# Chunk 0's queries and keys laid out by pairs of token blocks, in a new order of the pieces

## The chip, the cores and the metric

The kernel runs on one core of a Trainium2 chip. The metric is the device time of one execution in microseconds (us). The engines are TensorE (PE, its weight loads PEld), VectorE (DVE), ScalarE (ACT), GpSimd (POOL) and the DMA queues, which SP, ACT and POOL feed.

## What is computed

The input is one sequence of S = 2048 tokens with D = 640 features. It is normalized once, and two branches read the result: a sliding attention of 32 heads of 20 features, in which a token looks at itself and at 7 earlier tokens, each two positions further back (W = 8, dilation 2), and a feed-forward net of 1536 units with GELU. Both results and x are added.

```python
xn = layernorm(x)                                   # no gain or bias
q, k, v = split(xn @ wqkv)                          # 32 heads of 20
idx = pos[:, None] - 2 * arange(8)[None, :]         # masked where idx < 0
logits = einsum("bhsd,bhswd->bhsw", q, k[idx]) * 20 ** -0.5
attn = softmax(where(idx >= 0, logits, -1e9))
A = einsum("bhsw,bhswd->bhsd", attn, v[idx]) @ wo
B = gelu(xn @ w1 + b1) @ w2 + b2
out = x + A + B
```

## The kernel before

**Tiling.** Tokens are handled in 4 chunks of 512 (n = 0 to 3), each of 4 blocks of 128 (j or bl). Features lie on the 128 partitions in KT = 5 tiles. Everything is bfloat16 except sums in PSUM and the softmax. Queries, keys and values of a chunk are tiles [128, 5, 512], keys and values with 14 leading columns (PAD) more, which hold the last columns of the chunk before (zeros in chunk 0).

**Attention of a chunk.** VectorE multiplies queries with shifted keys: `qk n j h` (L402) handles token block j and four of the eight shifts (half h), writing `half0` or `half1`, 2560 elements per partition. The keys are read through a hand-made access pattern (`window`) that steps back by two columns from shift to shift. TensorE sums the products over the features of each head (`lg n`, L443) into the PSUM tile L, VectorE takes the maximum (`m`) and subtracts it (`mx`), ScalarE takes the exponential (`ex`), VectorE sums, inverts and multiplies (`ss`, `ri`, `at`). DMAs spread the weights over the partitions (`xd n` issued by SP for blocks 0 and 1, `xs n` by ScalarE for blocks 2 and 3). VectorE multiplies them with the values (`av n j h`) and adds up (`ad n`, `ot n`). In chunks 2 and 3 `pa` adds pairs of feature tiles first.

**Feed-forward net and output.** `f1n_t` (L549) is the first layer for unit tile t into a PSUM buffer, `ge n_t` its GELU on ScalarE. `o n bl pc` (L585, L587) is the output of a block: pc 0 to 3 from the net, pc 4 from the attention (`ot` must be done). `oc` copies it out of PSUM, `od` adds it to the output by a POOL DMA. The last block's output is added by VectorE and stored by SP and ACT.

**Chunk 0.** Its projections come in parts. `ga`, `gb`, `gd` make the queries of blocks 0 and 1, copied by `gc`. `hj w p g` makes queries, keys or values (w = 0, 1, 2) of pair p of token blocks (pair 0 is blocks 0 and 1) for feature tiles 0-1, 2-3 or 4 (g = 0, 1, 2), ten matmuls or five; `hc w p g` (L372) copies it out on ScalarE. In the other chunks a projection `pj n w t` is five matmuls of 512 columns, copied by `pc`. `pad n w` copies the leading columns.

**Normalization.** `st` are statistics on VectorE (chunks 0, 1); `su`, `ng`, `sq` do the same on ScalarE (chunks 2, 3). `rs` is the root on ScalarE, `rc` the reciprocal on VectorE, `xn` the normalized block, `tp`/`tc` its transpose (chunk 0 on TensorE; for the others `tc` is a DMA transpose on the SP queue). `ldx`, `ld2`, `ldo` are later loads on SP, `xp` copies x to the output, `xb` adds the bias there.

**Order.** The text `ORDER` lists all pieces in one line of time. Each engine of PE, DVE, ACT and SP executes its own pieces strictly in that order; waits between engines are found from the data, tile by tile and range by range. The pool `psA` has four PSUM buffers for `hj`, `pj`, `f1` (and for part of the last chunk's output): a buffer comes free when ScalarE has copied it out. L has one buffer, and so has each half of the output (`lo`, `hi`). ScalarE loads a function table (L167) whenever the next function is of another kind: root, exponential, GELU.

Of the kernel before, what the change touches and what calls it, by code (L numbers as in the profile page):

```python
# [13 lines left out]
BF16 = mybir.dt.bfloat16  # L14
F32 = mybir.dt.float32

S, D, F, H, W, DIL = 2048, 640, 1536, 32, 8, 2
P = 128
DH = D // H
PAD = (W - 1) * DIL  # L20
KT, FT = D // P, F // P
CH = 512
# [14 lines left out]

ORDER = """
pad01 pad02 st00a st00 sum1 rs00 mean1 neg1 rc00 sq1 xn00a xn00b tp00a wa tp00b wb tc00a rs01 ga tc00b rc01 xn01 gb2
tp01 gb3 tc01a tc01b gb4 gd gc0 ge tb b1 ho hj102 st02a gc1 st03a hc102 gc4 st02 rs02 st03 hj100 rs03 rc02 hc100 rc03  # L40
xn02 xn03 hj101 st12a hc101 st11a st13a hj201 st10a tp02 tc02 tp03 hj200 tc03 st11 hc201 hc200 hj202 hc202 hj012 hj110
hc110 st12 st13 st10 rs1 hc012 qk001 hj010 hc010 hj111 rc1 xn12 qk000 qk011 qk010 xn11 hj011 hc011 tc12 tc11 hj112
hc111 hc112 f10_1 ge0_1 qk020 xn13 tc13 qk030 f10_11 qk031 f10_6 ge0_6 xn10 f10_0 ge0_0 pad11 f10_9 hj211 hc211 ge0_9
f10_2 hj212 qk021 lg0 hc212 ge0_11 tc10 pj103 ge0_2 pc103 mask m0 mx0 ex0 ss0 pj114 pj101 pc101 pj104 pc104 pj111
pj113 pc114 pj112 pj102 pc111 ri0 ldx ld2 su23 pj100 pc113 pj110 at0 su21 pc112 su20 f11_0 pc102 pc100 pc110 qk110
qk101 qk130 f11_7 qk111 qk131 qk120 qk100 f10_4 xd0 su22 ng2 ge1_7 sq20 f11_3 ge1_3 ge1_0 f10_5 sq22 qk121 pj122 ge0_5
sq21 ldo ge0_4 hj210 xp0 xs0 f10_3 ge0_3 pj121 sq23 rs2 rc2 o000 o001 lg1 hc210 av010 av000 m1 xn21 f10_7 tc21 pc122
f11_9 av001 xn22 av030 tc22 mx1 pc121 ge0_7 f10_10 ge0_10 f10_8 pj123 xn20 tc20 ge0_8 xn23 ge1_9 f11_10 f11_5 ge1_5
o002 pj120 av020 av021 ex1 ss1 pc120 xp1 av031 ri1 pj124 pc124 o003 av011 pad21 tc23 pj213 pc213 pc123 pj202 pc202
pj211 pc211 pj214 pc214 at1 pj222 pad12 ge1_10 pc222 pj204 pj224 pc224 xs1 pj200 ad01 ad00 pc200 pj201 su31 ad02 ot0  # L50
xd1 pc201 pj210 pc210 av111 av110 su30 pj223 pc223 av131 av101 f11_4 pc204 pj203 f12_9 su32 pc203 xb1 su33 av130 pj221
pc221 o004 oc00 xb0 od00 pj220 pc220 o020 av121 o021 o022 o023 o024 ng3 sq31 sq30 sq32 oc02 f11_2 av120 av100 sq33 rs3
rc3 xn33 tc33 od02 xn30 o030 o031 o032 o033 ad10 tc30 o034 oc03 pj212 o010 ge1_4 ad11 ad12 o011 o012 o013 o014 xn31
tc31 f11_6 pc212 qk221 xn32 ge1_2 ot1 qk201 qk200 f12_4 ge2_4 qk210 qk211 qk230 qk231 ge1_6 pa210 oc01 qk220 pa211
pa200 pad22 f11_1 ge1_1 f12_11 ge2_11 pa201 tc32 pj314 pc314 pj300 pc300 pj303 pc303 pj301 pc301 ge2_9 pj304 pc304
pj311 pj302 pj313 pc313 pc302 pj312 pc312 f13_8 pj310 f13_10 pad31 pc310 f13_6 xl lg2 ge3_8 m2 mx2 ge3_10 pc311 ge3_6
o130 qk300 ex2 ss2 f13_5 f11_8 ge1_8 od03 f12_7 o131 qk310 ri2 ge2_7 pa300 at2 qk301 f12_1 pj324 qk321 qk331 qk311
ge3_5 f11_11 ge1_11 pa311 ge2_1 f13_11 o132 o133 pc324 f12_0 ge2_0 qk330 pj321 f13_1 xs2 qk320 pa310 f13_7 ge3_1 ge3_7
xp2 pj320 f13_9 ge3_9 o134 oc13 pc321 pc320 ge3_11 pj323 pc323 o110 pa301 o111 o112 lg3 m3 av230 av231 o113 od01 o114
oc11 mx3 pad32 av221 ex3 ss3 xd2 av210 ri3 av201 pj322 pc322 f13_0 at3 f13_3 ge3_3 o100 od11 o101 f12_5 o102 o103 o104  # L60
oc10 f13_2 o120 o121 xs3 ge3_2 av211 o122 av200 av220 ad21 ge2_5 od13 f12_6 ge3_0 o123 o124 xb2 xb3 ad20 f12_3 ad22
ot2 f12_2 oc12 ge2_6 ge2_2 f12_8 ge2_8 ge2_3 od12 f13_4 f12_10 o310 av321 ge3_4 o220 o221 o222 ge2_10 o223 o224 oc22
od10 od22 o330 o311 xd3 o200 o201 av330 o202 o203 av300 o204 oc20 od20 o331 o332 o210 o211 o212 o213 o214 oc21 av310
o312 o230 o231 o232 o233 o234 o313 av311 av331 av320 av301 ad31 ad30 ad32 oc23 ot3 o320 o321 o322 o323 o324 o314 od21
oc32 od23 o300 o301 o302 o303 o304 oc31 od32 o333 o334 od31 oc30 od30 oclo ohi ochi ochd
""".split()


# [1 line left out]
def kernel(  # L70
# [16 lines left out]
    nc = tc.nc  # L87
# [14 lines left out]
    qkvp = ctx.enter_context(tc.tile_pool(name="qkvp", bufs=2))  # L102
    prodp = ctx.enter_context(tc.tile_pool(name="prodp", bufs=1))
    smp = ctx.enter_context(tc.tile_pool(name="smp", bufs=1))
# [33 lines left out]
    for c in range(2):  # L138
        cs = slice(c * F // 2, (c + 1) * F // 2)
# [31 lines left out]
    mask = consts.tile([H, W, MW], BF16, name="mask")  # L171
# [20 lines left out]
    tiles = {}  # L192

    def get(key, make):
        if key not in tiles:
            tiles[key] = make()
        return tiles[key]
# [107 lines left out]
    def qkv_tile(n, which):  # L305
        if which == 0:
            return get(("q", n), lambda: qkvp.tile([P, KT, CH], BF16, tag="qT", name="qT"))
        tag = "kT" if which == 1 else "vT"
        return get((tag, n), lambda: qkvp.tile([P, KT, PAD + CH], BF16, tag=tag, name=tag))

    wqkv_p = [w[:].rearrange("p t (c r) -> p t r c", r=KT) for w in wqkv]

# [13 lines left out]
    def bank(key):  # L326
        return get(("bank", key), lambda: psA.tile([P, BPC, P], F32, tag="acc", name="gps"))
# [20 lines left out]
                q_piece(1, to, ti, ti == 0 and to == 0, ti == KT - 1 and to >= BPC - 1)  # L348

    def do_gc(g):  # L350
        q = qkv_tile(0, 0)
        if g == BPC:
            nc.scalar.copy(q[:, BPC, 0 : 2 * P].rearrange("p (b m) -> p b m", b=2), bank(BPC)[:, 0:2, :])
        else:
            nc.scalar.copy(q[:, 0:BPC, g * P : (g + 1) * P], bank(g)[:])
# [12 lines left out]
                )  # L368

    def do_gq(which, pair, a, b):  # L370
        off = (PAD if which else 0) + pair * 2 * P
        nc.scalar.copy(qkv_tile(0, which)[:, a:b, off : off + 2 * P], tiles["pair", which, pair, a][:, 0 : b - a, :])  # L372

    def do_pc(n, which, to):
        dest = qkv_tile(n, which)
        off = 0 if which == 0 else PAD
        nc.scalar.copy(dest[:, to, off : off + CH], tiles["pps", n, which, to][:])  # L377

    def do_pad(n, which):
        dest = qkv_tile(n, which)  # L380
        if n == 0:
            nc.gpsimd.memset(dest[:, :, 0:PAD], 0.0)
        else:
            nc.scalar.copy(dest[:, :, 0:PAD], qkv_tile(n - 1, which)[:, :, CH : CH + PAD])


    half = [prodp.tile([P, W // 2, KT, CH], BF16, name=f"half{i}") for i in range(2)]

    def window(src, h, cs):

        first = PAD - DIL * (W // 2 * h) + cs.start
        row = src[:, :, first : first + cs.stop - cs.start]
        (part, n_part), (tile_step, n_tile), (_, n_col) = row.ap
        return bass.AP(
            tensor=row.tensor,
            offset=row.offset,
            ap=[[part, n_part], [-DIL, W // 2], [tile_step, n_tile], [1, n_col]],
        )

    def do_qk(n, j, h):  # L400
        cs = slice(j * P, (j + 1) * P)
        nc.vector.tensor_tensor(  # L402
            out=half[h][:, :, :, cs],
            in0=qkv_tile(n, 0)[:, :, cs].unsqueeze(1).to_broadcast([P, W // 2, KT, P]),
            in1=window(qkv_tile(n, 1), h, cs),
            op=ALU.mult,
        )

# [75 lines left out]
            nc.vector.tensor_tensor(out=a[:, 0:k, :], in0=a[:, 0:k, :], in1=a[:, k : 2 * k, :], op=ALU.add)  # L484

    def do_recip(n):
        rs = smp.tile([P, P], F32, tag="rs", name="rs")
        tiles["rs", n] = rs
        nc.vector.reciprocal(rs[:], tiles["ss", n][:, 0, :])

# [133 lines left out]
    def piece(name, fn, *args):  # L624
        assert name not in pieces
        pieces[name] = lambda: fn(*args)

    for name in "tb b1 mean1 ho ldx ld2 ldo xl oclo ohi ochi ochd mask".split():
        piece(name, locals()[f"do_{name}"])
    for u, a, b, eng, own in (("a", 0, 2, "ve", "lo"), ("b", 2, KT, "se", "hi")):  # L630
        piece(f"xn00{u}", do_xn, 0, 0, a, b)
# [24 lines left out]
    for g in (0, 1, BPC):  # L656
        piece(f"gc{g}", do_gc, g)
    for which in range(3):
        for pair in range(0 if which else 1, 2):
            for g, (a, b) in enumerate(COLS):  # L660
                piece(f"hj{which}{pair}{g}", do_gp, which, pair, a, b)
                piece(f"hc{which}{pair}{g}", do_gq, which, pair, a, b)
    for n in range(NCH):
# [18 lines left out]
        for which in (1, 2):  # L682
            piece(f"pad{n}{which}", do_pad, n, which)
# [3 lines left out]
        for h in range(2):  # L687
            for j in range(BPC):
                piece(f"qk{n}{j}{h}", do_qk, n, j, h)
                piece(f"av{n}{j}{h}", do_av, n, j, h)  # L690
            if n in PAIRED:
                for c in range(2):
                    piece(f"pa{n}{h}{c}", do_pa, n, h, c)
        piece(f"lg{n}", do_lg, n)
        for name, fn in (("m", do_max), ("mx", do_sub), ("ex", do_exp), ("ss", do_sum), ("ri", do_recip), ("at", do_attn)):
            piece(f"{name}{n}", fn, n)
# [54 lines left out]
```

## Time and profile before

| quantity | value |
|---|---|
| median of 3 runs | 215.12 us (214.79 to 215.48) |
| the profiled execution | 215.14 us |
| its span, first to last instruction | 212.6 us |
| TensorE busy | 205.3 us (97%) |
| VectorE busy | 174.2 us (82%) |
| ScalarE busy | 126.3 us (59%) |
| mean granted TensorE clock | 0.998 |

The span is counted from the first instruction; some 2.5 us of the profiled execution's time lie outside it. Busy shares are averages over the span. In timeline rows the columns are start, duration, engine, line, operation, tiles, shape, count, and in brackets the idle time ahead with what ended it. Rows of one group overlap a little where an engine starts the next instruction before the last has fully ended, so the step from start to start is shorter than the duration of one.

### The profile page before, as it was taken

Reading aid. Unit: us, or ns where it says so; the run is one execution under the profiler, and the core shown is the slowest. Engines: PE = TensorE matmul, PEld = TensorE weight load, DVE = VectorE, ACT = ScalarE, POOL = GpSimd, SP = SyncE. Lnnn points to the kernel's source line nnn. Section 1 sums busy time; section 2 is a strip of 40 time slices with the busy share of each in tenths; the row PEclk is TensorE's granted clock in tenths of the full one; section 3 lists DMA queues with packets and bytes.
Section 4 is the critical chain, followed back from the end, with each engine's and each line's share of the span. In section 5 each row is a group of like instructions: output and inputs, shape, how many; then the busy total and the mean of one; then the engine's idle time right before and its main releaser. Section 6 shows DMA issues by size and latency. Waiting matters only on the chain.

```text
span 212.6 us, 3291 instructions
## 1 busy us (share of the span) xinstructions
PE 205.3 (97%) x1327; PEld 114.6 (54%) x1349; DVE 174.2 (82%) x162; ACT 126.3 (59%) x241; POOL 19.8 (9%) x37
## 2 busy tenths in 40 slices
PE   8999799999999999999999999999999999999993
PEld 3999355545445555555545544544555555555552
DVE  3498885639889999999999969996999999999001
ACT  5576686989998778678875477435462641111120
POOL 2000000000200200110110000006101101111121
PEclk9999999999999999999999999999999999999999
DMA  6992248977692395024611000396924611122253
GB/s 213 390 396 83 63 63 256 363 165 245 111 173 65 123 174 147 0 34 62 111 19 28 0 0 0 62 274 124 192 44 72 166 21 12 22 31 34 31 62 62
DMA packets 24069, 23.89 MB, mean 112 GB/s; under 512 B 9080, under 2 KB 21880, under 8 KB 24056
## 3 DMA queue, kind: packets, MB, share of 16 engines
q1 hardware_dynamic: 17008, 14.68, 23.5%
q0 software_dynamic: 4144, 4.92, 17.9%
q10 hardware_dynamic: 2904, 4.10, 6.4%
q8 instruction: 10, 0.16, 0.3%
q14 instruction: 3, 0.02, 0.0%
HBM read 10.00 MB, written 7.54 MB: 82 GB/s over the span
## 4 chain that ended last, share of the span: by engine, by line
PE 86%; DVE 8%; ACT 3%; issue 1%; DVEq 0%
PE lo L585 26%; PE pps L318 22%; PE hps L549 19%; DVE half L402 8%; PE hi L587 8%; PE gps L362 4%; PE L L443 3%; PE idle L415 2%; PE gps L331 1%; ACT hT L565 1%; ACT xn L257 1%; PE tp L274 1%; ACT L167 1%; ACT kT L372 0%; ACT kT L377 0%
## 5 line engine op out<-in xcount | busy, mean ns | idle before, releaser
L549 PE MATMUL hps<-xnT,w_sb 128*128 128x512 bf16 x237 | 55.6, 379 | 1.8 <-ACT kT L372 1.4
L402 DVE TENSOR_TENSOR half<-qT,kT 128x2560 bf16<-128x2560 bf16 x32 | 45.8, 1486 | 5.3 <-ACT kT L377 3.6
L585 PE MATMUL lo<-w_sb,hT 128*128 128x512 bf16 x136 | 39.7, 379 | 0.1
L549 PEld LDWEIGHTS <-w_sb 128*128 128x128 bf16 x240 | 23.0, 98 | 28.7 <-issue 2.9
L587 PE MATMUL hi<-w_sb,hT 128*128 128x128 bf16 x144 | 31.5, 219 | 0.5 <-issue 0.2
L592 ACT CAST osb<-lo 128x512 bf16<-128x512 f32 x15 | 8.8, 585 | 39.1 <-issue 19.9
L565 ACT ACTIVATE hT<-hps,b1T 128x512 bf16<-128x512 f32 x36 | 23.9, 684 | 8.9 <-PE hps L549 8.9
L528 DVE TENSOR_TENSOR half<-vT,ax 128x2560 bf16<-128x2560 bf16 x16 | 23.1, 1476 | 1.5 <-PE L L443 1.5
L598 POOL DMA_DIRECT2D out_dram<-osb x15 | 13.0, 864 | 118.6 <-ACT osb L593 106.7
L585 PEld LDWEIGHTS <-hT 128*128 128x128 bf16 x144 | 14.1, 98 | 17.5 <-issue 0.8
L528 DVE TENSOR_TENSOR half<-vT,x_sb 128x2560 bf16<-128x2560 bf16 x16 | 22.6, 1484 | 0.0
L585 PE MATMUL lo<-wo,oT 128*128 128x512 bf16 x76 | 22.4, 379 | 0.0
L537 DVE TENSOR_TENSOR half<-half,half 128x5120 bf16<-128x5120 bf16 x8 | 22.2, 2820 | 0.1
L167 ACT ACT_TABLE_LOAD x14 | 18.0, 1283 | 1.0 <-PEq L735 0.7
L318 PE MATMUL pps<-xnT,wv_sb 128*128 128x512 bf16 x73 | 18.2, 379 | 0.1
L318 PE MATMUL pps<-xnT,wk_sb 128*128 128x512 bf16 x75 | 18.0, 379 | 0.1
L318 PE MATMUL pps<-xnT,wq_sb 128*128 128x512 bf16 x72 | 17.4, 379 | 0.1
L587 PE MATMUL hi<-wo,oT 128*128 128x128 bf16 x80 | 16.9, 219 | 0.2
L587 PEld LDWEIGHTS <-hT 128*128 128x128 bf16 x144 | 14.1, 98 | 1.7
L585 PEld LDWEIGHTS <-oT 128*128 128x128 bf16 x80 | 7.8, 98 | 9.4
L318 PEld LDWEIGHTS <-wq_sb 128*128 128x128 bf16 x75 | 8.7, 118 | 7.6 <-issue 0.4
L318 PEld LDWEIGHTS <-wk_sb 128*128 128x128 bf16 x75 | 8.7, 118 | 7.3
(86 smaller groups left out, 267.0 us busy)
## 6 DMA issues: line engine op xcount, KB each, us to landing
w_sb<-in_B_w_dram SPq DMA_DIRECT2D x4, 960.0 KB, 10.8
out_dram<-osb POOLq DMA_DIRECT2D x15, 160.0 KB, 3.4
out_dram<-b2bc POOLq DMA_DIRECT2D x3, 640.0 KB, 6.8
x_sb<-in_A_x_dram SPq DMA_DIRECT2D x1, 1280.0 KB, 6.0
out_dram<-x_sb ACTq DMA_DIRECT2D x1, 1120.0 KB, 4.9
ax<-attn SPq DMA_DIRECT2D x4, 256.0 KB, 4.0
ax<-attn ACTq DMA_DIRECT2D x4, 256.0 KB, 4.2
x_sb<-attn SPq DMA_DIRECT2D x4, 256.0 KB, 4.7
```

Source lines behind the costliest of these rows:

```text
L167: nc.scalar.activation(warm[:], nc.const_aps.tensor(0.0, [P, 1], F32), func)
L318: nc.tensor.matmul(ps[:], lhsT=wqkv_p[which][:, ti, to, :], rhs=xnT[:, ti, :], start=(ti == 0), stop=(ti == KT - 1),)
L362: nc.tensor.matmul(ps[:, to - a, :], lhsT=wqkv_p[which][:, ti, to, :], rhs=tiles["xnT", 0][:, ti, pair * 2 * P : (pair + 1) * 2 * P], star ...
L402: nc.vector.tensor_tensor(out=half[h][:, :, :, cs], in0=qkv_tile(n, 0)[:, :, cs].unsqueeze(1).to_broadcast([P, W // 2, KT, P]), in1=window ...
L528: nc.vector.tensor_tensor(out=half[h][:, :, :, cs], in0=window(qkv_tile(n, 2), h, cs), in1=ax_view(n)[:, j, ws, :].unsqueeze(2).to_broadca ...
L537: nc.vector.tensor_tensor(out=a, in0=a, in1=b, op=ALU.add)
L549: nc.tensor.matmul(ps[:], lhsT=w1_sb[:, ti, ft * P : (ft + 1) * P], rhs=tiles["xnT", n][:, ti, :], start=(ti == 0), stop=(ti == KT - 1),)
L565: nc.scalar.activation(hT, tiles["hps", n, ft][:], ACT.Gelu_apprx_tanh, bias=b1T[:, ft : ft + 1], scale=1.0)
L585: nc.tensor.matmul(lo[:], lhsT=lhs, rhs=rhs[:, 0:CH], start=first, stop=last)
L587: nc.tensor.matmul(hi[:, 0 : D - CH], lhsT=lhs, rhs=rhs[:, CH:D], start=first, stop=last)
L592: nc.scalar.copy(osb[:, 0:CH], tiles["lo", n, bl][:])
L598: nc.gpsimd.dma_start(rows, tiles["osb", n, bl][:], accum_op=ALU.add)
```

## The change

In chunk 0 the query tile is read as two ranges, one for each pair of token blocks, [128, 5, 256] each. The key tile becomes two ranges of [128, 5, 14 + 256], each with leading columns of its own; those of pair 1 are a copy of the last 14 columns of pair 0, made by the new piece `pk` on ScalarE. `qk` of chunk 0 reads queries and keys from the range of its pair. The tiles of the other chunks are laid out as before. The reciprocal's tile takes the tag, and so the buffer, of the maximum. The order of the pieces is new throughout.

```diff
 ORDER = """
 pad01 pad02 st00a st00 sum1 rs00 mean1 neg1 rc00 sq1 xn00a xn00b tp00a wa tp00b wb tc00a rs01 ga tc00b rc01 xn01 gb2
-tp01 gb3 tc01a tc01b gb4 gd gc0 ge tb b1 ho hj102 st02a gc1 st03a hc102 gc4 st02 rs02 st03 hj100 rs03 rc02 hc100 rc03
-xn02 xn03 hj101 st12a hc101 st11a st13a hj201 st10a tp02 tc02 tp03 hj200 tc03 st11 hc201 hc200 hj202 hc202 hj012 hj110
-hc110 st12 st13 st10 rs1 hc012 qk001 hj010 hc010 hj111 rc1 xn12 qk000 qk011 qk010 xn11 hj011 hc011 tc12 tc11 hj112
-hc111 hc112 f10_1 ge0_1 qk020 xn13 tc13 qk030 f10_11 qk031 f10_6 ge0_6 xn10 f10_0 ge0_0 pad11 f10_9 hj211 hc211 ge0_9
-f10_2 hj212 qk021 lg0 hc212 ge0_11 tc10 pj103 ge0_2 pc103 mask m0 mx0 ex0 ss0 pj114 pj101 pc101 pj104 pc104 pj111
-pj113 pc114 pj112 pj102 pc111 ri0 ldx ld2 su23 pj100 pc113 pj110 at0 su21 pc112 su20 f11_0 pc102 pc100 pc110 qk110
-qk101 qk130 f11_7 qk111 qk131 qk120 qk100 f10_4 xd0 su22 ng2 ge1_7 sq20 f11_3 ge1_3 ge1_0 f10_5 sq22 qk121 pj122 ge0_5
-sq21 ldo ge0_4 hj210 xp0 xs0 f10_3 ge0_3 pj121 sq23 rs2 rc2 o000 o001 lg1 hc210 av010 av000 m1 xn21 f10_7 tc21 pc122
...
+tp01 gb3 tc01a tc01b gb4 gd gc0 ge tb b1 st03a gc1 hj101 hj100 hj202 st02a hc101 st03 rs03 st02 rs02 gc4 hc100 hj201
+ho rc03 hc202 rc02 xn02 xn03 tp02 tc02 tp03 st12a st11a hj200 hj102 st13a st10a tc03 st13 hc201 hc102 hj010 pk st12
+hj012 hc200 hc010 st11 hj011 st10 rs1 hc012 qk001 rc1 qk000 hc011 qk010 qk011 hj112 hc112 xn12 tc12 xn13 tc13 hj110
+hc110 hj111 hc111 qk020 qk021 f10_6 ge0_6 xn11 tc11 f10_0 f10_2 f10_9 f10_1 ge0_0 hj212 ge0_9 f10_11 xn10 tc10 ge0_2
+ldx hj211 qk030 ld2 qk031 lg0 hc212 hc211 pad11 ge0_1 pj100 ge0_11 pc100 mask m0 mx0 ex0 ss0 ri0 pj102 pc102 pj112
+pc112 pj101 pj111 pc101 pj104 at0 pj103 pj114 su20 su21 pc104 pc111 su22 pj110 pc114 pc110 pc103 pj113 pc113 qk130
+qk100 qk111 qk120 qk131 qk101 qk110 qk121 xs0 pj124 pc124 su23 hj210 hc210 pj121 pc121 f11_9 ng2 sq20 pj122 pc122 sq21
+sq23 pj120 pj123 f10_5 ldo o000 pc123 sq22 pc120 rs2 rc2 f10_7 f10_10 lg1 m1 av031 xd0 av001 av011 av000 mx1 ge0_5
+av030 xn23 tc23 ge0_7 f10_4 xn22 tc22 f10_3 ge0_4 ge0_10 ge0_3 xn20 tc20 ge1_9 xn21 f10_8 ge0_8 f11_5 ge1_5 f11_10
+pad21 ge1_10 av010 f11_0 ge1_0 ex1 ss1 av021 ri1 o001 f11_7 o002 tc21 av020 xp1 pj203 pc203 su33 pj211 at1 xp0 xd1
+pj201 pj202 ad00 pc211 pc201 f11_3 ge1_3 pj214 pc214 o003 ge1_7 pad12 pj213 pc213 ad01 ad02 ot0 pj212 pc212 av101
+pj224 pc224 pj222 xs1 pj204 pc204 pc222 pad22 av110 pj220 pj210 av131 pc220 su30 av100 xb0 av111 av121 av120 xb1 pc210
+pj223 av130 su31 su32 ng3 pj200 pc202 sq32 f12_2 o004 oc00 od00 sq33 pj221 pc223 pad31 o020 o021 o022 pc200 pc221 sq30
+o023 o024 oc02 sq31 rs3 rc3 xn31 tc31 f12_11 xn32 ad10 tc32 o030 o031 o032 o033 o034 oc03 f11_6 ad11 ad12 qk211 o010
+o011 o012 o013 o014 f12_4 ge2_11 ot1 qk221 qk231 qk201 qk200 xn33 tc33 xn30 qk220 qk230 qk210 ge2_2 pa201 ge2_4 ge1_6
+f11_11 pa200 f11_2 ge1_2 tc30 pj311 pj302 pc302 pj304 pc311 ge1_11 pa211 pa210 pj310 pj312 pc312 pj323 pc323 pj300
+pc304 pj314 pc314 pj313 pc313 pc310 od03 pj303 f13_0 pj301 pc300 f13_5 xl pc301 pc303 pj321 lg2 m2 pc321 ge3_5 ge3_0
+oc01 od01 f11_4 ge1_4 qk321 mx2 f11_1 qk320 od02 ge1_1 ex2 f11_8 ss2 f13_8 ge1_8 pj324 pj320 o130 ge3_8 f12_1 ri2 at2
+xd2 o131 f12_9 ge2_9 qk310 o132 o133 o134 qk311 ge2_1 qk301 xs2 qk331 pa310 oc13 od13 f13_11 qk300 f13_4 qk330 ge3_4
+ge3_11 o110 o111 o112 o113 pa300 pj322 o114 pa301 pc320 oc11 f12_0 pa311 lg3 m3 mx3 ex3 av231 xp2 ss3 o100 o101 o102
+o103 o104 pc322 pc324 oc10 f12_5 ri3 at3 xd3 f13_6 ge3_6 o120 ge2_5 f13_2 f12_6 ge2_0 f13_10 o121 o122 od10 f13_1 o123
+o124 av220 av201 xb2 xb3 ge3_1 ge3_2 av200 oc12 od12 f13_9 ge3_9 ge3_10 ge2_6 f12_8 ge2_8 xs3 f13_3 ge3_3 av221 av211
+av210 f12_7 ge2_7 av230 f12_10 f12_3 ge2_3 f13_7 ge3_7 o220 o330 ad20 o331 pad32 ad21 ad22 o221 o222 ot2 av331 ge2_10
+o223 o224 oc22 od22 o310 o230 o231 o232 o233 o234 av320 oc23 av330 av300 av301 av311 o311 od11 o200 o201 o202 o203
+o204 av321 oc20 od20 o312 o210 o211 o212 o213 o214 oc21 av310 ad30 od21 ad31 o313 o320 o321 o322 ad32 ot3 o323 o324
+od23 o314 oc32 o300 o301 o302 o303 o304 od32 o332 o333 o334 ohi oc31 od31 oc30 oclo ochi ochd od30
 """.split()
...
@@ -305,8 +305,20 @@
     def qkv_tile(n, which):
         if which == 0:
             return get(("q", n), lambda: qkvp.tile([P, KT, CH], BF16, tag="qT", name="qT"))
-        tag = "kT" if which == 1 else "vT"
-        return get((tag, n), lambda: qkvp.tile([P, KT, PAD + CH], BF16, tag=tag, name=tag))
+        if which == 2:
+            return get(("vT", n), lambda: qkvp.tile([P, KT, PAD + CH], BF16, tag="vT", name="vT"))
+        flat = get(("kT", n), lambda: qkvp.tile([P, 2 * KT * (PAD + 2 * P)], BF16, tag="kT", name="kT"))
+        return flat[:, 0 : KT * (PAD + CH)].rearrange("p (t m) -> p t m", t=KT)
+
+    def pair_of(which, pair):
+
+        if which == 0:
+            return qkv_tile(0, 0)[:].rearrange("p t m -> p (t m)")[:, pair * KT * 2 * P : (pair + 1) * KT * 2 * P].rearrange(
+                "p (t m) -> p t m", t=KT
+            )
+        qkv_tile(0, 1)
+        size = KT * (PAD + 2 * P)
+        return tiles["kT", 0][:, pair * size : (pair + 1) * size].rearrange("p (t m) -> p t m", t=KT)
 
     wqkv_p = [w[:].rearrange("p t (c r) -> p t r c", r=KT) for w in wqkv]
 
@@ -348,7 +360,7 @@
                 q_piece(1, to, ti, ti == 0 and to == 0, ti == KT - 1 and to >= BPC - 1)
 
     def do_gc(g):
-        q = qkv_tile(0, 0)
+        q = pair_of(0, 0)
         if g == BPC:
             nc.scalar.copy(q[:, BPC, 0 : 2 * P].rearrange("p (b m) -> p b m", b=2), bank(BPC)[:, 0:2, :])
         else:
@@ -368,8 +380,13 @@
                 )
 
     def do_gq(which, pair, a, b):
-        off = (PAD if which else 0) + pair * 2 * P
-        nc.scalar.copy(qkv_tile(0, which)[:, a:b, off : off + 2 * P], tiles["pair", which, pair, a][:, 0 : b - a, :])
+        if which == 2:
+            off = PAD + pair * 2 * P
+            dest = qkv_tile(0, which)[:, a:b, off : off + 2 * P]
+        else:
+            off = PAD if which else 0
+            dest = pair_of(which, pair)[:, a:b, off : off + 2 * P]
+        nc.scalar.copy(dest, tiles["pair", which, pair, a][:, 0 : b - a, :])
 
     def do_pc(n, which, to):
         dest = qkv_tile(n, which)
@@ -377,11 +394,16 @@
         nc.scalar.copy(dest[:, to, off : off + CH], tiles["pps", n, which, to][:])
 
     def do_pad(n, which):
-        dest = qkv_tile(n, which)
+        dest = pair_of(1, 0) if (n, which) == (0, 1) else qkv_tile(n, which)
         if n == 0:
             nc.gpsimd.memset(dest[:, :, 0:PAD], 0.0)
+        elif (n, which) == (1, 1):
+            nc.scalar.copy(dest[:, :, 0:PAD], pair_of(1, 1)[:, :, 2 * P :])
         else:
             nc.scalar.copy(dest[:, :, 0:PAD], qkv_tile(n - 1, which)[:, :, CH : CH + PAD])
+
+    def do_pk():
+        nc.scalar.copy(pair_of(1, 1)[:, :, 0:PAD], pair_of(1, 0)[:, :, 2 * P :])
 
 
     half = [prodp.tile([P, W // 2, KT, CH], BF16, name=f"half{i}") for i in range(2)]
@@ -399,10 +421,13 @@
 
     def do_qk(n, j, h):
         cs = slice(j * P, (j + 1) * P)
+        q, k, at = qkv_tile(n, 0), qkv_tile(n, 1), cs
+        if n == 0:
+            q, k, at = pair_of(0, j // 2), pair_of(1, j // 2), slice(j % 2 * P, (j % 2 + 1) * P)
         nc.vector.tensor_tensor(
             out=half[h][:, :, :, cs],
-            in0=qkv_tile(n, 0)[:, :, cs].unsqueeze(1).to_broadcast([P, W // 2, KT, P]),
-            in1=window(qkv_tile(n, 1), h, cs),
+            in0=q[:, :, at].unsqueeze(1).to_broadcast([P, W // 2, KT, P]),
+            in1=window(k, h, at),
             op=ALU.mult,
         )
 
@@ -484,7 +509,7 @@
             nc.vector.tensor_tensor(out=a[:, 0:k, :], in0=a[:, 0:k, :], in1=a[:, k : 2 * k, :], op=ALU.add)
 
     def do_recip(n):
-        rs = smp.tile([P, P], F32, tag="rs", name="rs")
+        rs = smp.tile([P, P], F32, tag="m", name="rs")
         tiles["rs", n] = rs
         nc.vector.reciprocal(rs[:], tiles["ss", n][:, 0, :])
 
@@ -625,7 +650,7 @@
         assert name not in pieces
         pieces[name] = lambda: fn(*args)
 
-    for name in "tb b1 mean1 ho ldx ld2 ldo xl oclo ohi ochi ochd mask".split():
+    for name in "tb b1 mean1 ho ldx ld2 ldo xl oclo ohi ochi ochd mask pk".split():
         piece(name, locals()[f"do_{name}"])
     for u, a, b, eng, own in (("a", 0, 2, "ve", "lo"), ("b", 2, KT, "se", "hi")):
         piece(f"xn00{u}", do_xn, 0, 0, a, b)
```

## Prediction

> **What bounds the kernel now.** I read the page first (busy shares, then the chain that ended last), then TensorE's own waits, then the stretches of five microseconds, and at the one place that stood out the timeline.
>
> ```profile
> span 212.6 us, 3291 instructions
> PE 205.3 (97%) x1327; PEld 114.6 (54%) x1349; DVE 174.2 (82%) x162; ACT 126.3 (59%) x241; POOL 19.8 (9%) x37
> ...
> PE 86%; DVE 8%; ACT 3%; issue 1%; DVEq 0%
> ```
>
> TensorE is busy for 97% of the span and carries 86% of the chain. The change adds and removes no matmul, so only time in which TensorE stands still can be won, and any new standstill is lost in full. TensorE's list of waits names one that matters:
>
> ```profile
> PE hps L549 <- ACT kT L372: 1.4, 1, 1.4
> ```
>
> The stretches put it early; from 35 us to 205 us TensorE is full:
>
> ```profile
> 20.00:25.00 5.00, 3.67 (x23) 2.31 (x23) 4.37 (x4) 2.76 (x5) 0.00 (x0) 1.00 0.29 66
> 25.00:30.00 5.00, 4.74 (x25) 2.55 (x25) 4.67 (x4) 4.97 (x9) 0.00 (x0) 1.00 0.14 34
> ...
> 35.00:40.00 5.00, 5.00 (x25) 2.70 (x23) 3.48 (x5) 4.46 (x8) 0.00 (x0) 1.00 1.06 394
> ```
>
> (Columns: stretch, its length, busy time of PE, PEld, DVE, ACT, POOL, then granted clock.) The timeline of that place shows the cause:
>
> ```profile
> 18.42 1.49 DVE L402 TENSOR_TENSOR half<-qT,kT 128x2560 bf16<-128x2560 bf16 x1 [0.83 <-ACT kT L372]
> 20.11 4.29 DVE L402 TENSOR_TENSOR half<-qT,kT 128x2560 bf16<-128x2560 bf16 x3
> 21.87 0.56 ACT L372 CAST qT<-gps 128x512 bf16<-128x512 f32 x1
> 24.44 0.86 ACT L372 CAST kT<-gps 128x512 bf16<-128x512 f32 x2 [2.01 <-DVE half L402]
> 25.07 3.60 PE L549 MATMUL hps<-xnT,w_sb 128*128 128x512 bf16 x15 [1.35 <-ACT kT L372]
> 25.33 5.70 DVE L402 TENSOR_TENSOR half<-qT,kT 128x2560 bf16<-128x2560 bf16 x4 [0.93 <-ACT kT L372]
> 31.92 2.34 PE L443 MATMUL L<-half,head_of 128*32 128x512 bf16 x40
> ```
>
> The first four products (`qk001` to `qk010`) read keys of pair 0. They end at 24.40, and only then may ScalarE write the keys of pair 1 (`hc111`, `hc112`), which they do not need. The pairs' columns alternate in memory for all five tiles, so the reader's span covers the other pair. While `hc111` waits, ScalarE passes nothing on, the four PSUM buffers fill, and TensorE stops for 1.35 us. Likewise the first product waits 0.83 us, until `hc110` ends at 18.31. The queries show no such link: at 21.87 ScalarE writes queries of pair 1 in the middle of three products. So the keys' layout does the work, and the queries' layout I cost at nothing.
>
> **The wait removed.** On TensorE, from 9.84 to the first matmul of `lg0` at 31.92, 22.08 us pass. Starts lie 0.216 us apart at 512 columns, 0.109 at 256, 0.056 at 128 (five of 512 make the 1.08 us steps of the chain; thirty of 256 take 3.29). Ahead of `lg0` stand 9 pieces hj of ten matmuls (9 x 1.093 = 9.84), 5 of five (2.73), 10 transposes (0.56) and 6 FFN pieces (6 x 1.079 = 6.47): 19.60 us. So 22.08 - 19.60 = 2.48 us are waits. The new order has the same pieces ahead of `lg0`, differently sorted, so it can start at 9.84 + 19.60 + 0.09 (entry, as before) = 29.53, if two others keep up.
>
> VectorE: its statistics end at 17.59 as before. `hc102`, now the last copy that `qk001` needs, ends at about 16.45 (its matmuls end at 15.87), so `qk001` starts at 17.6. With a step of 1.41 us per product and 0.3 for `rc1`, the eighth ends at 29.3, against 31.02; `qk020` wants `hc111`, due at 22.3, at 23.6. ScalarE: copies step by 0.5, `xn` by 0.81, GELUs by 0.58, a table load with its warm-up by 1.40. Its queue then reads `hc112` 19.7, `xn12`, `xn13` 21.3, `hc110`, `hc111` 22.3, table and `ge0_6` 24.3, `xn11`, `ge0_0` 25.7, `ge0_9` 26.4, `xn10`, `ge0_2` 27.8. Each frees a PSUM buffer 0.5 to 1.3 us before TensorE wants it. The transpose `tc10` can be issued at 27.3, its data wanted at 31.8; transposes landed in 2.4 to 4.5 us. So 2.39 us come off.
>
> **Small parts.** `pk`, one copy of 128x70, is added to ScalarE: 0.24 us by the same-sized copy at 30.05. Behind it stand `hc200` and `hc010`, whose buffers are wanted 0.9 us later or more; it is covered, and without that cover costs 0.24. Maximum and reciprocal in one buffer: both are written and read by VectorE alone, and in its queue `mx` precedes `ri` and `at` precedes the next `m`, so nothing waits. Product speed: 1.486 us for 2560 elements before. Rows now lie 270 elements apart instead of 526. The nearest slow row is a subtraction of float32, 1.23 us for 1024 elements, which scaled gives 3.1. The value rows, of the other 526-element tile, also take 1.48, so I keep 1.49. The Trainium skill (VectorE: DVE Perf Modes, "Mode 2×_1P") asks for 16-bit data, step one and 4-byte alignment; rows of 540 bytes and a pair offset of 2700 bytes still satisfy that, so by its rule this term is nought too; did it fail, the sum would go to the last rival below.
>
> A removed TensorE pause might also pay in clock. The granted clock stays 1.00 through the 1.35 us pause, and the next matmuls start 0.216 apart, so I count no such gain.
>
> **Does the rest of the order keep 2.39 us?** I moved all marks by that much and added up queue by queue. `lg1` needs `qk121`. TensorE reaches it at 54.2, VectorE delivers at 54.7: a stall of 0.3, as before (56.47 against 57.15). From the end of `lg1`, VectorE needs 26.9 us to `ot0` (2 x 1.14 for m and mx, 8 x 1.41, 1.38, 0.88, 1.13, three adds of 2.78, 1.41), and TensorE has 27.6 us ahead of `o004`: no stall. `lg2`: halves 120.8, TensorE 121.1. `lg3`: 145.0 against 145.3. `o224`: `ot2` 173.7 against 174.5. `o324`: `ot3` 194.8 against 196.3; TensorE then has 10.7 us left. All are met, by 0.3 to 1.5 us. Thinner places are PSUM buffers behind ScalarE. `pj210` needs `pc204`, now queued behind the two DMA issues of `xs1` (2.02 us before): 0 to 0.6, I take 0.1. `f12_1` needs `ge1_8`, behind `ex2` and two table loads: 0 to 0.7, I take 0.2, as sums meet within that. `f13_7` needs `ge3_3`, behind the issues of `xs3` (2.63 us before): 0 to 1.3, I take 0.3, since issues partly overlap ScalarE's work at 51.67. `pj203` needs transpose `tc21`, due at 64.8 to 66.9, wanted at 66.2: 0 to 0.7, I take none, as the median landing is 2.5. On SP, `ldo` now precedes `xd0` and `xp0` follows the transposes; both are wanted 10 us later than issued. The last store moves with TensorE's end: `od30` is issued 3.3 us ahead of it instead of 2.7, so it cannot be last. Given back: 0.6.
>
> Sum against the profiled execution, 215.14 us (span 212.6 and 2.5 around it; the median of three is 215.12): 215.14 - 2.39 + 0.6 = 213.35, say 213.3. The thin places at their dear ends (0.6 + 0.7 + 1.3 + 0.7 = 3.3 instead of 0.6) would give 216.0, but they do not add up, since a TensorE late at one finds the next buffer free. One or two of them give 214.4. At their cheap ends, with `lg1` unstalled, it is 212.5.
>
> **Rivals.** *Gain eaten*: the later stages take the 2.4 us back in several tie places, 214.5 to 215.7, centre 215.1. For it: six ties within half a microsecond. Against: VectorE idles for 1.64 and 2.13 us ahead of its third and fourth maximum already, and a late TensorE relaxes every tie.
>
> *ScalarE falls behind around `lg1`* (the one that ends slower): `f11_9`, `f10_5`, `f10_7` and `f10_10` hold all four PSUM buffers when `lg1` starts, and `ge0_5`, which frees the first, stands behind four squares, six copies, the root's table and the GELU table. At the steps above ScalarE is through `ge0_4` at 58.9, wanted by `f10_8` at 59.2. At full row durations (copies 0.59, squares 0.83 + 0.20, sums 0.95, GELUs 0.69, xn 0.92, DMA issues 2.63 for 1.25) the same list is 3.65 us longer, TensorE loses 3.3, and the time is 216.6. It decides against the change once ScalarE needs 2.75 us more than my steps. Against it: the steps come from back-to-back runs of the same instructions, and fourteen table loads have a mean of 1.283 us.
>
> The Trainium skill (ScalarE: Activation LUTs, "Rules for kernel authors") speaks against this place: it budgets some 2.7 us for every switch to another table set. With two switches in that list its figure, an estimate here, would add 2.6 us to ScalarE, and the sum would be 215.6 instead of 213.3; I keep the trace's 1.28 and the warm-up behind it.
>
> *The link stays*: if the two key pairs are still held to touch, `hc112` waits for `qk011` (23.7 instead of 19.4), `hc111` ends at 26.9, the products at 32.6, `lg0` starts 3.2 us later than I say, and the time is 216.5. Against it: the pairs now lie in two ranges that do not meet.
>
> *Products slow down*: eight at 3.1 instead of 1.49 make `lg0` 13 us later: 226.
>
> **How the numbers follow.** Forecast 213.3 with 0.74, own range 212.5 to 214.4. Gain eaten 0.09. ScalarE behind 0.11, link stays 0.05, slow products 0.01. A change under 0.3%, 0.65 us, cannot be told from none. So faster 0.74, same 0.09, slower 0.17. Leaving out the tails of the forecast and the slower ends, the range is 212.5 to 216.0.
>
> **What would show it.** Right: no wait of ScalarE's kT copies for VectorE's products, `lg0` near 29.5 us, VectorE's eight products without a gap from 17.6, TensorE's slices full from 20 us on, span near 210.8. Wrong: a hole on TensorE between 55 and 66 us (ScalarE), a copy of keys still ended by L402 (link), products above 1.49 us, or holes at 80, 130 or 169 us larger than 0.6.

## The result: 211.65 us, and the profile after

| quantity | before | after |
|---|---|---|
| median, same chip | 214.99 us (214.79 to 215.48, 4 runs) | 211.65 us (211.64 to 211.69, 4 runs) |
| ratio | 1 | 0.9842 [0.9824, 0.9860] |
| the profiled execution | 215.14 us | 211.66 us |
| its span | 212.63 us | 209.38 us |
| first matmul of `hj` to first matmul of `lg0` | 22.08 us | 19.72 us |
| first matmul of `lg0` to start of the last matmul | 177.11 us | 177.13 us |
| the end: start of the last matmul to the start of the last instruction | 3.55 us | 2.94 us |

The forecast was 213.3 us, its range 212.5 to 216.0. The time lies 0.85 us below the range: the direction and the mechanism ahead of `lg0` held, the gain was larger than any case had it. The profile after, its first lines and the chain that ended last:

```profile
span 209.4 us, 3294 instructions
PE 204.5 (98%) x1327; PEld 114.4 (55%) x1349; DVE 174.6 (83%) x162; ACT 125.2 (60%) x240; POOL 19.7 (9%) x37
...
PE 95%; ACT 2%; issue 1%; DVE 0%
```

VectorE's 8% of the chain are gone; TensorE carries 95%. Its busy time is almost what it was, so what went is standstill. The whole list of what TensorE waits for (waited for: us in total, times, longest):

```profile
PE idle L440 <- PEq L760: 0.8, 1, 0.8
PE hps L574 <- ACT hT L590: 0.2, 1, 0.2
```

The wait for ScalarE's copy of keys is not in it. The stretches, one of them late (columns as in the prediction; the two behind the clock are the DMA's busy share and its GB/s):

```profile
20.00:25.00 5.00, 4.95 (x30) 2.87 (x29) 5.00 (x5) 4.97 (x9) 0.00 (x0) 1.00 0.30 67
25.00:30.00 5.00, 5.00 (x44) 3.10 (x46) 3.69 (x3) 3.48 (x8) 0.00 (x0) 1.00 0.42 72
125.00:130.00 5.00, 4.84 (x25) 2.44 (x24) 4.66 (x6) 4.94 (x8) 0.00 (x0) 1.00 0.27 32
```

TensorE is busy for 4.95 us of the stretch from 20 us, where it was 3.67. The timeline of that place:

```profile
16.20 0.25 ACT L406 COPY kT<-kT 128x70 bf16<-128x70 bf16 x1
17.15 1.45 DVE L427 TENSOR_TENSOR half<-qT,kT 128x2560 bf16<-128x2560 bf16 x1
18.80 9.90 DVE L427 TENSOR_TENSOR half<-qT,kT 128x2560 bf16<-128x2560 bf16 x7
20.97 1.06 ACT L389 CAST kT<-gps 128x512 bf16<-128x512 f32 x2
29.26 2.34 PE L468 MATMUL L<-half,head_of 128*32 128x512 bf16 x40
```

The eight products run without a gap from 17.15 to 28.70, at the old speed (1.484 us each on average over all 32 products, 1.486 before). ScalarE copies the keys of pair 1 at 20.97 in the middle of them and waits for none. `lg0` starts at 29.26.

### The profile page after: what moved, and what is told of

The parts are those of the page before. It is cut to its first block, busy times and chain, and to the rows that moved or that the text cites. A ratio compares the mean times of both kernels' runs of the same rounds, so it can differ in the third digit from the quotient of the medians.

```text
span 209.4 us, 3294 instructions
## 1 busy us (share of the span) xinstructions
PE 204.5 (98%) x1327; PEld 114.4 (55%) x1349; DVE 174.6 (83%) x162; ACT 125.2 (60%) x240; POOL 19.7 (9%) x37
## 4 chain that ended last, share of the span: by engine, by line
PE 95%; ACT 2%; issue 1%; DVE 0%
PE lo L610 27%; PE hps L574 24%; PE pps L330 22%; PE hi L612 8%; PE gps L374 7%; PE L L468 4%; PE idle L440 2%; PE gps L343 1%; ACT L167 1%; PE tp L274 1%; ACT hT L590 1%; ACT e L501 0%; ACT warm L167 0%; DVE osb L640 0%; PE tb L450 0%
## 5 line engine op out<-in xcount | busy, mean ns | idle before, releaser
L574 PE MATMUL hps<-xnT,w_sb 128*128 128x512 bf16 x233 | 55.0, 379 | 0.5 <-ACT hT L590 0.2
L610 PE MATMUL lo<-w_sb,hT 128*128 128x512 bf16 x139 | 40.4, 379 | 0.1
L574 PEld LDWEIGHTS <-w_sb 128*128 128x128 bf16 x240 | 22.8, 98 | 26.9 <-issue 1.1
L330 PE MATMUL pps<-xnT,wv_sb 128*128 128x512 bf16 x72 | 17.7, 379 | 0.1
```

The lines of the kernel that those rows point to most:

```text
L330: nc.tensor.matmul(ps[:], lhsT=wqkv_p[which][:, ti, to, :], rhs=xnT[:, ti, :], start=(ti == 0), stop=(ti == KT - 1),)
L574: nc.tensor.matmul(ps[:], lhsT=w1_sb[:, ti, ft * P : (ft + 1) * P], rhs=tiles["xnT", n][:, ti, :], start=(ti == 0), stop=(ti == KT - 1),)
L610: nc.tensor.matmul(lo[:], lhsT=lhs, rhs=rhs[:, 0:CH], start=first, stop=last)
```

## Where the profiled 3.48 us went

- From the first `hj` to `lg0`: 22.08 - 19.72 = 2.36 us less (forecast 2.39).
- From `lg0` to the last matmul: 0.02 us more (forecast 0.6 more). TensorE pauses about 0.3 us ahead of 129.8, and a pause of 0.29 us at `lg1` is gone.
- Behind the last matmul: 3.55 - 2.94 = 0.61 us less (forecast none).
- Ahead of the first `hj`: it starts at 9.54 instead of 9.84, 0.30 us less. The work there is the same in every kernel of this study, and over its 13 profiles this start lies between 9.21 and 10.29. It follows when TensorE's full clock is granted and when the weights land. In the seven profiles in which TensorE has no pause in that stretch, it moves with the clock, from 9.21 (full clock from 5.01) to 9.84 (from 6.80); in others TensorE waits up to 0.6 us for `wq_sb`. I put it down to the execution.
- Outside the span: 2.51 before, 2.28 after, 0.23 us less. Over the profiles it is 2.05 to 2.57; I have no cause for it.

Together 2.36 - 0.02 + 0.61 + 0.30 + 0.23 = 3.48 us. Some 2.95 us of it belong to the kernel.

## The experiments

Unless another base is named, an edit is to the changed kernel.

**Layout and order apart.** `order_only` is the kernel before with the new order, without `pk`:

```diff
 # the kernel before
-ORDER = the old order
+ORDER = the new order without pk
```

> The new order with the old layout of queries and keys (no pk, no shared buffer). Theory, the keys' layout matters: the copies hc110 and hc111 of pair 1 write inside the span that the first four products read, so hc110 waits for qk011, some 1.4 us longer than in the changed kernel; table load, GELUs and xn10 behind it come some 2 us later, TensorE stops ahead of hj211, lg0 starts near 31.1 instead of 29.26, and the time is near 213.5 us. The copy hc112 lies behind the end of that span and should not wait. Rival, the order alone does it: no wait of kT copies for products, lg0 at 29.3, 211.7 us.

Measured: 213.35 us (212.92 to 213.92), ratio 0.9926 [0.9900, 0.9952]. From the waits of `order_only` over all engines:

```profile
ACT kT L372 <- DVE half L402: 2.1, 1, 2.1
```

and the two rows with keys of pair 1 from its timeline of ScalarE:

```profile
19.53 0.37 ACT L372 CAST kT<-gps 128x256 bf16<-128x256 f32 x1
23.64 1.07 ACT L372 CAST kT<-gps 128x512 bf16<-128x512 f32 x2 [2.11 <-DVE half L402]
```

With the old layout the new order has the same false wait, 2.11 us of it. TensorE pauses four times between 23.6 and 30.2 (0.61, 0.42, 0.31, 0.31). From `hj` to `lg0` it takes 21.38 us, 1.66 more than the changed kernel. The order alone is worth 0.70 us here, and 0.63 behind the last matmul (2.92 us). One detail went against my rival "the link stays": the copy of the small group, `hc112` at 19.53, does not wait at all. Only the two copies of the larger groups do.

`layout_only` has the new layout and the old order:

```diff
-ORDER = the new order
+ORDER = the old order, with "hc101 pk st11a" for "hc101 st11a"
```

> The new layout in the old order, pk put behind hc101. Theory: no kT copy waits for a product, the first product starts at 17.6 instead of 18.42, TensorE's 1.5 us pause at 23.3 and most of the small ones up to 30 us are gone, lg0 near 29.6, and the time is near 212.8 us: the layout is worth 2.2 us, the order's other moves 0 to 0.5 and the last stores 0.5. Rival, the order does it: the pause stays in another place, less than 0.7 us is won, 214.5 us or more.

Measured: 212.65 us (212.56 to 212.75), ratio 0.9892 [0.9866, 0.9917]. Its timeline of VectorE and of ScalarE:

```profile
17.35 1.45 DVE L427 TENSOR_TENSOR half<-qT,kT 128x2560 bf16<-128x2560 bf16 x1
...
21.34 0.87 ACT L389 CAST kT<-gps 128x512 bf16<-128x512 f32 x2
```

No wait stands in brackets behind the copies of keys, and `hj` to `lg0` takes 19.71 us: the same as with both parts (19.72). So the layout by itself makes the whole 2.36 us there, and the reordering ahead of `lg0` adds nothing to it. What the new order adds to the layout is behind the last matmul: 3.59 us in `layout_only`, 2.94 in the changed kernel.

**Keys or queries.** `keys_only` leaves the queries in the old layout:

```diff
 if which == 0:
-    return the range of the pair, [128, 5, 256]
+    return qkv_tile(0, 0)[:, :, pair * 2 * P : (pair + 1) * 2 * P]
```

> The changed kernel, with the queries of chunk 0 in the old layout. Theory: the queries' layout removes no wait, lg0 starts at 29.3 and the time is 211.65 us, within 0.2. Rival, the queries were linked too: a wait of qT copies for products appears, lg0 later by 0.5 us or more, 212.2 us or more.

Measured: 211.75 us (211.63 to 212.09), ratio 0.9853 [0.9830, 0.9875]. No copy of queries waits for a product. `lg0` comes 20.17 us after `hj`; some 0.4 of that is a wait for the transfer of `wv_sb`, up to 11.95, the rest of the timeline runs as in the changed kernel. The queries' layout costs and brings nothing that these runs can tell, as predicted.

**The end of the kernel.** The prediction counted nothing behind the last matmul. `tail_back` moves one piece of three matmuls back to where the old order has it, which delays `od30`, the last large accumulating store, against the two final stores:

```diff
-... oc32 o300 o301 o302 o303 o304 od32 o332 o333 o334 ohi ...
+... oc32 o332 o300 o301 o302 o303 o304 od32 o333 o334 ohi ...
```

> The changed kernel with the three matmuls of o332 put back ahead of o300, as in the kernel before, so that the last POOL store od30 is issued 0.65 us nearer to the end. Theory: od30's packets then overlap the two last stores of SP and ACT again, from the last matmul to the end of the span 3.3 us pass instead of 2.7, and the time is near 212.2 us. Rival, the end only moves with the last matmul: 211.65 us, 2.7 us.

Measured: 212.23 us (211.86 to 212.36), ratio 0.9871 [0.9851, 0.9891]. That is 0.48 us more than `keys_only` beside it, which ends like the changed kernel; in the profiles the end takes 3.51 us instead of 2.94, 0.57 more, and `lg0` to the last matmul is 177.14. The issues and the landings, changed kernel first (timeline rows, then in a second view queue, KB and median us from issue to landing):

```profile
204.36 0.86 POOL L623 DMA_DIRECT2D out_dram<-osb  x1 [3.76 <-ACT osb L618]
206.48 0.37 SPq L632 DMA_DIRECT2D out_dram<-osb  x1
```

```profile
out_dram<-osb SPq DMA_DIRECT2D x1, 128.0 KB, 1.8
out_dram<-osb ACTq DMA_DIRECT2D x1, 32.0 KB, 1.5
```

The same two views of `tail_back`:

```profile
205.15 0.86 POOL L623 DMA_DIRECT2D out_dram<-osb  x1 [4.41 <-ACT osb L618]
206.62 0.36 SPq L632 DMA_DIRECT2D out_dram<-osb  x1
```

```profile
out_dram<-osb SPq DMA_DIRECT2D x1, 128.0 KB, 2.4
out_dram<-osb ACTq DMA_DIRECT2D x1, 32.0 KB, 2.1
```

The kernel before had its `od30` at 207.65 and SP's store at 209.12; its landings:

```profile
out_dram<-osb SPq DMA_DIRECT2D x1, 128.0 KB, 2.3
out_dram<-osb ACTq DMA_DIRECT2D x1, 32.0 KB, 2.0
```

A lead of 1.47 us (before, `tail_back`) goes with landings of 2.3 or 2.4 and 2.0 or 2.1; a lead of 2.12 us with 1.8 and 1.5. Before, the packets of `od30` end at 210.69, 0.42 us after SP's first packet at 210.27; after, they end at 207.38 against 207.34. Over all 13 profiles this goes together. Where `od30`'s packets lie over SP's first one by 0.36 to 0.47 us (before, `layout_only`, `tail_back`), that first packet starts 1.13 to 1.18 us behind its issue, and SP's packets are spread over 0.77 to 0.89 us. With an overlap of 0.14 us or less it is 0.86 to 0.87 and 0.53 to 0.64. The store of `od30` does not end last, it slows the ones that do. Then the same move should pay without the rest of the change. `before_tail` does it to the kernel before:

```diff
 # the kernel before
-... o330 o331 o332 o210 ... od32 o333 ...
+... o330 o331 o210 ... od32 o332 o333 ...
```

> The kernel before with one edit: the three matmuls of o332 moved from before o210 to behind o304, beside o333. Theory: od30 is issued 0.65 us earlier against the end, its packets no longer overlap the last two stores; lg0 to the last matmul stays 177.1 us, from the last matmul to the end 2.9 us pass instead of 3.55, and the time falls by 0.6 us, to 214.2 us beside 214.8 us of the kernel before. Rival: what the changed kernel's end won comes from other moves of the order, 214.8 us.

Measured: 214.33 us (214.10 to 214.80, 12 runs) beside 214.94 (17 runs), ratio 0.9972 [0.9958, 0.9987]. The lead is 2.12 us, and the landings in its DMA issues are:

```profile
out_dram<-osb SPq DMA_DIRECT2D x1, 128.0 KB, 1.8
out_dram<-osb ACTq DMA_DIRECT2D x1, 32.0 KB, 1.5
```

The end takes 2.92 us. In this profile TensorE also loses 0.39 us in small pauses between `lg0` and the last matmul (177.50 instead of 177.11), a loss that no expectation had; whether the other executions share it is not shown. The medians differ by 0.61.

**ScalarE's reserve at `lg1`.** My rival that ended slower rested on ScalarE being nearly late there, with 0.3 us to spare. `late_1` and `late_4` add one and four unused squares ahead of `pc120`:

```diff
+def do_xx(i): nc.scalar.activation(trash[:], x_sb[:, 0, :], ACT.Square)
-... pj123 f10_5 ldo o000 pc123 sq22 pc120 ...
+... pj123 f10_5 ldo o000 pc123 sq22 xx pc120 ...      # late_4: four of them
```

> The changed kernel with one more square of 128x640 on ScalarE, put ahead of the copy pc120, in the list that has to be worked off around lg1 (its result is not used; 0.83 us, with its wait for the one before 0.95). Theory of the prediction's rival: the list has some 0.3 us to spare, so TensorE stands 0.5 to 0.7 us longer between 55 and 60 us and the time is near 212.25 us. Rival: ScalarE is busy for 60% only and takes it in, 211.65 us.

> The same with four squares, 3.3 to 3.8 us of ScalarE. Theory: past the spare 0.3 us every microsecond on ScalarE is one on TensorE, which stands 3.0 to 3.4 us longer, and the time is near 214.85 us, about that of the kernel before. Rival: ScalarE catches up in its gaps and less than half is lost, below 213.3 us.

Measured: `late_1` 212.48 us (212.11 to 213.45), ratio 0.9891 [0.9860, 0.9921]; TensorE has three new pauses between 56.2 and 59.2 (0.11, 0.30 and 0.31 us), and `lg0` to the last matmul takes 177.84, 0.71 more. The square and the copy `pc120` behind it, then the same copy in the changed kernel (timelines of ScalarE):

```profile
51.32 0.74 ACT L741 ACTIVATE trash<-x_sb 128x640 bf16<-128x640 bf16 x1
51.96 0.57 ACT L394 CAST vT<-pps 128x512 bf16<-128x512 f32 x1
```

```profile
51.52 0.57 ACT L394 CAST vT<-pps 128x512 bf16<-128x512 f32 x1
```

Counted from the first `hj` (9.21 and 9.54), the copy comes at 42.75 instead of 41.98. So the square cost ScalarE 0.77 us and TensorE 0.71: only some 0.06 us were spare, not the prediction's 0.3. The changed kernel's own rows say the same: `ge0_4` ends at 58.66, and `f10_8`, which wants the buffer that it frees, starts at 58.76. That `late_1` still loses what was expected is luck, since the square was shorter than the 0.95 us counted for it.

`late_4` 215.06 us (214.72 to 216.26), ratio 1.0010 [0.9991, 1.0029]; `lg0` to the last matmul takes 180.83, 3.70 more. Its copy `pc120`, its timeline of TensorE, and the stretches there:

```profile
54.52 0.57 ACT L395 CAST vT<-pps 128x512 bf16<-128x512 f32 x1
```

```profile
55.13 1.48 PE L575 MATMUL hps<-xnT,w_sb 128*128 128x512 bf16 x5 [2.16 <-ACT vT L395]
56.55 3.73 PE L469 MATMUL L<-half,head_of 128*32 128x512 bf16 x40
```

```profile
52.50:55.00 2.50, 0.47 (x3) 0.10 (x1) 1.90 (x2) 2.44 (x4) 0.00 (x0) 1.00 0.00 0
55.00:57.50 2.50, 2.37 (x17) 0.81 (x20) 0.34 (x2) 2.45 (x5) 0.00 (x0) 0.70 0.00 0
57.50:60.00 2.50, 2.50 (x36) 0.88 (x28) 0.00 (x0) 2.49 (x5) 0.00 (x0) 0.62 0.00 0
```

TensorE pauses for 2.16 us ahead of 55.13, and from 55.99 on the granted clock is one half for 3.41 us: `lg1` takes 3.73 us instead of 2.59 in the changed kernel. The copy comes 3.08 us later than in the changed kernel, counted from the first `hj` (here at 9.46). Less the 0.06 that was spare, that makes 3.02 us of waiting; the other 0.68 of the 3.70, by subtraction, goes with the clock. The ten executions agree: the six with a mean clock of 0.99 took 215.06 to 216.26 us, the four with 1.00 took 214.72 to 214.80, some 3.1 above the changed kernel. Four squares thus give back all that the change won, most of it by waiting. The rival's place and mechanism exist; the change stays on the good side of them by less than 0.1 us.

**The one pause left.** TensorE's 0.2 to 0.3 us ahead of 129.8 is `f12_1`, which wants the buffer that `ge1_8` frees. The changed kernel's timeline of ScalarE there:

```profile
126.65 1.01 ACT L501 ACTIVATE e<-L 128x1024 bf16<-128x1024 f32 x1
127.67 1.28 ACT L167 ACT_TABLE_LOAD   x1
...
129.08 0.67 ACT L590 ACTIVATE hT<-hps,b1T 128x512 bf16<-128x512 f32 x1
```

The GELU that frees it stands behind the exponential and a table load. `o131_first` gives TensorE something else to do:

```diff
-... o130 ge3_8 f12_1 ri2 at2 xd2 o131 f12_9 ...
+... o130 ge3_8 o131 f12_1 ri2 at2 xd2 f12_9 ...
```

> The changed kernel with o131 ahead of f12_1. Theory: TensorE's last pause that a buffer causes, 0.32 us at 129.4 (f12_1 waits for the buffer of ge1_8), is filled by the 0.82 us of o131; from lg0 to the last matmul 176.8 us pass instead of 177.13, and the time is near 211.35 us. Rival: the pause moves to f12_9 or to lg3, 211.65 us.

`both_moves` has this and one more piece moved to the end, to lengthen the lead of `od30`:

```diff
-... o330 ad20 o331 pad32 ... od32 o332 o333 ...
+... o330 ad20 pad32 ... od32 o331 o332 o333 ...       # and o131 as above
```

> The same, and o331 put next to o332 behind o304, so that od30 is issued another 0.65 us earlier against the end. Theory: in the changed kernel od30's packets end as the first of SP's last store start, so a longer lead gives 0.0 to 0.1 more: near 211.3 us, with 2.8 to 2.95 us from the last matmul's start to the end. o224 and o324 come 0.65 us earlier, and ot2 and ot3 are still done in time. Rival: the longer lead gives as much as the first 0.65 us did, 0.6 us: 210.75 us; or ot2 is late and the time grows.

Measured side by side: `o131_first` 211.58 us (211.30 to 212.41), ratio 0.9851 [0.9825, 0.9876]; `both_moves` 211.79 us (211.69 to 212.03), 0.9854 [0.9831, 0.9877]. `o131_first` brings `lg0` to the last matmul to 176.81, 0.32 less. `both_moves` eats that again: `o224` then waits for VectorE's `ot2` up to 173.34, 0.37 us (177.19 in all), and the end takes 2.92 us as before the move, though the packets of `od30` now end 0.59 us before SP's first. A longer lead brings no more.

To see whether 0.32 us can be told from no change, the changed kernel and this one ran side by side once more, as `after_again` (nothing edited) and `o131_again` (the edit of `o131_first`).

> The changed kernel again, beside the next: 211.65 us, 177.13 us from lg0 to the last matmul, and a first hj between 9.2 and 10.3 us, which is by the execution and not by the kernel.

> The changed kernel with o131 ahead of f12_1, again: 176.81 us from lg0 to the last matmul, and a median 0.3 us below that of the changed kernel run beside it, 211.35 us. Rival: the spread of the first ten microseconds hides it, less than 0.1 us.

Measured: 212.24 us (211.72 to 212.81, 6 runs), ratio 0.9876 [0.9850, 0.9903], and 211.21 us (210.85 to 211.91, 5 runs), ratio 0.9833 [0.9806, 0.9859]. The intervals overlap. `lg0` to the last matmul is 177.13 and 176.81 again, so 0.32 us is the edit. The medians differ by 1.03; in the two profiles the rest is the beginning (9.56 against 9.31) and what lies outside the span (2.52 against 2.05). The changed kernel, measured twice, has medians of 211.65 and 212.24.

## Why the prediction missed its range

**Right: ahead of `lg0`.** The false wait was the whole of the gain ahead of `lg0`: 2.36 us measured, 2.39 worked out, `lg0` at 29.26 against 29.5, eight products without a gap, at the old speed. `layout_only` and `order_only` show that it is the layout that takes it away, `keys_only` that the queries do not matter. `pk` (0.25 us) is hidden, and the shared buffer shows no wait. TensorE does not pause around `lg1`. This kernel's 13 table loads take 1.283 us each with 0.20 for the warm-up behind it, the trace's price that the prediction kept. The Trainium skill (ScalarE: Activation LUTs, "Rules for kernel authors") budgets some 2.7 us for every switch to another set, which this kernel did not pay.

**Wrong: ScalarE's reserve at `lg1`.** The prediction had 0.3 us, from 58.9 to 59.2; the runs show some 0.06 (`late_1`). The place was right, its margin was over-sized, and the change passed it by less than the errors of such a sum. The addition for `ot0` is off too (its terms make 26.7 us, not 26.9), without effect.

**Wrong: given back 0.6.** Of the thin places `pj210`, `f13_7` and `pj203` cost nothing, `f12_1` 0.3, and the stall at `lg1`, counted as unchanged, vanished. The net is 0.02, where the prediction had 0.6. The ties had been priced at a value inside their bounds one by one, and summed. Three of four landed at their cheap end, and a place that could gain was left at zero.

**Wrong: nothing behind the last matmul.** The step that failed is "it cannot be last", with the conclusion that the last store only moves with TensorE's end. It is true that `od30` is not last. Yet in the kernel before it lay 0.42 us over the packets of the stores that are, and a longer lead takes 0.6 us off the end, a term that the prediction put at nothing. Its lead was misread too: the 2.7 and 3.3 us run from the end of `o304`'s matmuls, before ScalarE has copied the result, while the rows have `od30` issued 1.47 and 2.12 us ahead of SP's store. That the final stores took 2.3 and 2.0 us to land could be read before; that an earlier `od30` would shorten this took a run to see.

**Wrong: the range.** The sum with the terms for the thin places and the end mended is 215.14 - 2.36 + 0.02 - 0.61 = 212.19 us. The measured 211.65 is still 0.5 us below. That is the beginning (0.30) and the part outside the span (0.23), which differ between executions. How far the time lies below the range is therefore partly luck: the profiled 215.14 us, from which the sum starts, lies 0.2 to 0.4 above the medians of the kernel before in the later measurements (214.77 to 214.94), and the changed kernel measured again took 212.24 us, 0.26 below the range instead of 0.85. The range had no width for this, and its lower end, with every tie cheap and `lg1` unstalled, still had nothing behind the last matmul.

**Open.** What the packets of `od30` share with the final stores is not shown, only that less overlap goes with faster landings; a single packet of SP's store takes 43 to 44 ns on average with and without overlap. Nor is it shown what sets the 2.05 to 2.57 us outside the span.

## What to carry to other kernels

Where waits are found by range, lay data so that one step's range does not reach over another's: the row of a copy that waits for a reader of other data showed 2.0 us, the layout alone won 2.36, and the new order alone only 0.7. Read the end of a kernel as a stage of its own: a large store issued 0.65 us earlier made the two final ones 0.5 us faster each. Give a range the spread of the start and of what lies outside the span, here half a microsecond each way, before the terms of the change.

## What the runs showed of the hardware

- In the profiled execution of `late_4` a TensorE pause of 2.2 us was followed by 3.41 us at half the granted clock; the 1.35 us pause of the kernel before was not (1.00 through it). The Trainium skill (TensorE: Matmul & The Clock Gate, "What's actually happening") lets the clock fall after at least one idle window of about 3.4 us. Here less than such a window of idleness sufficed, and the half clock lasted about one. It does not always come: six of ten executions have a mean clock of 0.99 and took 215.06 to 216.26 us, four have 1.00 and took 214.72 to 214.80.
- Two stores of 128 and 32 KB landed in 1.8 and 1.5 us nearly alone, and in 2.3 and 2.0 us where the last 0.42 us of a 160 KB accumulating store lay over them.
- With the old layout a copy into the last feature tile of the other pair did not wait (`hc112` in `order_only`), while copies into the tiles before it did. That fits a tracked range that reaches from the first to the last element of the access pattern, not over the whole tile.
